# A planned kernel that counts TensorE's instructions in blocks of 256 and takes values in two stretches of a batch

## The chip, the core and the metric

One of the eight cores of one Trainium2 chip runs the kernel. The metric is the device time in microseconds; before, three runs took 1141.72, 1147.73 and 1151.67 us, with a median of 1147.73. The engines are TensorE (PE, its weight loads PEld), VectorE (DVE), ScalarE (ACT), GpSimd (POOL), and SyncE (SP), whose queue issues nearly all transfers.

## The reference

Attention with two mixings of heads, then two perceptrons. All arrays are float32 apart from the perceptrons' weights, which are float64 and are cut to float32 on the chip.

```python
scores = scale * np.matmul(q, k.transpose(0, 1, 3, 2))      # 4 batches, 12 heads, 448 x 448, depth 64
scores = np.einsum('bhij,hg->bgij', scores, w_pre)          # first mixing
attn = softmax(scores)                                      # with its maximum, + 1e-9 below
attn = np.einsum('bhij,hg->bgij', attn, w_post)             # second mixing
x = (attn @ v) -> (1792, 768)
h = x @ w_in; x = (h * np.cos(h)) @ w_out                   # 768 -> 2048 -> 768
h = max(x @ w1, x @ w2, x @ w3); out = h @ w_out2           # 768 -> 768 -> 768
```

## The kernel before, in words

**Attention.** A batch's 448 query rows are cut into groups of 12, 12, 11 and 10 "slots" of 10 rows. For each group and each of six head pairs TensorE makes products of queries and keys (`qk`, L587) into two PSUM banks; VectorE or ScalarE copies each to SBUF (`evac`, L486), and SP sends it (`send`, L608) into a grid `t` in which heads lie along partitions. A "visit" is two slots of this grid: the first mixing (`mix1`, L617), the maximum (`rowmax`, L625, VectorE), the exponential (`soft`, L631, ScalarE), the reciprocal of the sum (L636, L640), the scaling of w_post by it (`wscale`, L645), the second mixing (`mix2`, L655) of 56 narrow matmuls in the trace, and a copy (`keep`, L486) of its result for each slot into `a2`. When all visits of one or more groups have been kept (a "half" in `HALVES`), TensorE multiplies them with the values, two head pairs at a time (`av`, L682 and L684: one take), VectorE adds the two parts (`addx`, L703), and SP writes them to `xT` in memory (`out`, L707). Every float32 matmul of the program is two weight loads and two matmuls in the trace, every fp32r matmul one and one.

**Perceptrons.** Weights are rebuilt from float64 (L259 to L270) and, as `xT` is, split into two fp32r parts (L135, L138, L150, L154); three matmuls (L163 to L165) make each product. The first layer of batch 0 may run among the last visits.

**What sets the order.** `attention` adds every step to a `Plan` with a rank, a time on each engine that may do it, what must come before it, and which buffers it takes. `Plan.run` (L393) is a list scheduler: it keeps a clock for each engine, looks at all steps whose predecessors are placed, takes of those that can start within `WAIT` = 0.034 us of the earliest the one with the lowest rank, and writes its instructions at once. The order of every engine's queue is therefore fixed when the program is built, and each engine works through its queue in that order. Before, a step on TensorE can start when TensorE is free and its inputs are there, and nothing else counts.

The lines that say which groups of slots share a half, batch by batch, and the ranks of a half's takes:

```python
HALVES = [[[10], [12], [12, 11]], [[10, 12], [12, 11]], [[10, 12], [12, 11]], [[12, 11], [12], [10]]]
...
r = last + RAV + RAVGAP * x * APO / 2
...
soon = min(c)[0] + WAIT
t, rank, n, key = min((x for x in c if x[0] <= soon), key=lambda x: x[1:3])
```

## Time and profile before

| | us |
|---|---|
| median of three runs | 1147.73 |
| profiled execution | 1149.56 |
| its span, first to last instruction | 1147.8 |
| TensorE busy (matmuls) | 1102.0 (96%) |
| VectorE busy | 932.4 (81%) |
| ScalarE busy | 670.1 (58%) |

The granted TensorE clock was 0.995 of full speed. Each engine works on its own queue, so a wait costs time only if it lies on the chain that ends last. A matmul's busy time overlaps that of its neighbours: what a group costs is read from the start of its first matmul to the start of what follows. "issue" as the cause of a wait means that the engine waited for nothing that the profile shows.

### The profile page before, as it was taken

How to read it: one execution, taken by the hardware profiler on the slowest of the kernel's cores; microseconds unless marked ns; L12 is line 12 of the kernel's file. 1: busy time of each engine (PE TensorE's matmuls, PEld its weight loads, DVE VectorE, ACT ScalarE, POOL GpSimd, SP SyncE). 2: the span in 40 equal slices, each digit the busy share in tenths (PEclk: the TensorE clock that was granted, in tenths of full speed). 3: DMA queues.
4: the chain of work that ended last, by engine and by line, in shares of the span. 5: the costliest groups of instructions: out<-in, count | busy, mean ns of one | idle time of the engine just before them, and what ended most of it. 6: DMA issues, size and time to landing. Idle time of an engine off the chain costs nothing.

```text
span 1147.8 us, 30574 instructions
## 1 busy us (share of the span) xinstructions
PE 1102.0 (96%) x12332; PEld 943.5 (82%) x12332; DVE 932.4 (81%) x2011; ACT 670.1 (58%) x1477; POOL 56.5 (5%) x51
## 2 busy tenths in 40 slices
PE   9789989999988999999999999999999999999998
PEld 4566657666766899999999999999999999999987
DVE  5778868887879999897979798956977779778994
ACT  4667757766767985555555555545634354445472
POOL 4000000000000000000000000000001021011120
PEclk9999999999999999999999999999999999999999
DMA  6675755765544765343535353300012211222233
GB/s 213 204 204 173 217 168 173 217 210 168 173 147 136 260 188 171 117 151 104 151 104 152 92 147 101 123 21 22 1 53 67 74 49 40 78 63 70 83 119 115
DMA packets 96365, 146.89 MB, mean 128 GB/s; under 512 B 12672, under 2 KB 78816, under 8 KB 96224
## 3 DMA queue, kind: packets, MB, share of 16 engines
q1 hardware_dynamic: 95968, 144.92, 41.6%
q8 instruction: 97, 1.59, 0.6%
q14 instruction: 44, 0.36, 0.1%
q0 software_dynamic: 256, 0.02, 0.0%
HBM read 85.74 MB, written 20.45 MB: 93 GB/s over the span
## 4 chain that ended last, share of the span: by engine, by line
PE 85%; DVE 5%; DMA 4%; issue 3%; ACT 2%; SPq 0%; ACTq 0%; DVEq 0%
PE ps L164 21%; PE ps L165 21%; PE ps L163 21%; PE aps L655 6%; PE ps L587 6%; PE mps L617 5%; PE aps L682 4%; DMA t<-s 1%; DMA v<-in_v_dram 1%; DVE x L336 1%; DVE nm L625 1%; PE aps L684 1%; DMA wraw<-in_w_dram 0%; DVE xs L703 0%; DMA q<-in_q_dram 0%
## 5 line engine op out<-in xcount | busy, mean ns | idle before, releaser
L165 PE MATMUL ps<-x,w 128*128 128x448 f32 x816 | 299.8, 367 | 5.7 <-DVE x L154 5.5
L163 PE MATMUL ps<-x,w 128*128 128x448 f32 x816 | 300.0, 368 | 1.8 <-ACT x L150 0.7
L164 PE MATMUL ps<-x,w 128*128 128x448 f32 x816 | 299.2, 367 | 0.4 <-DVE w L299 0.3
L165 PEld LDWEIGHTS ps<-x,w 128*128 128x128 f32 x816 | 153.2, 188 | 22.3 <-DVE x L154 9.0
L163 PEld LDWEIGHTS ps<-x,w 128*128 128x128 f32 x816 | 153.2, 188 | 16.8 <-ACT gh L925 1.0
L164 PEld LDWEIGHTS ps<-x,w 128*128 128x128 f32 x816 | 153.2, 188 | 14.2 <-DVE w L299 1.1
L631 ACT ACTIVATE e<-mps,nm 128x448 f32<-128x448 f32 (+1 forms) x184 | 115.4, 637 | 44.3 <-DVE nm L625 41.0
L163 PE MATMUL ps<-gh,w 128*128 128x448 f32 x384 | 140.9, 367 | 0.0
L164 PE MATMUL ps<-gh,w 128*128 128x448 f32 x384 | 140.7, 366 | 0.0
L165 PE MATMUL ps<-gl,w 128*128 128x448 f32 x384 | 140.5, 366 | 0.0
L655 PEld LDWEIGHTS aps<-w2s,e 60*64 60x64 f32 x5040 | 95.9, 135 | 41.1 <-issue 27.1
L296 ACT CAST w<-wf 128x384 fp32r<-128x384 f32 x168 | 81.2, 514 | 73.7 <-DVE wf L288 50.8
L625 DVE TENSOR_REDUCE nm<-mps 128x1 f32<-128x448 f32 (+1 forms) x184 | 108.0, 614 | 19.1 <-PE mps L617 18.0
L655 PE MATMUL aps<-w2s,e 60*64 60x60 f32 x5040 | 99.4, 220 | 21.3 <-issue 19.7
L587 PE MATMUL ps<-k,q 64*64 64x448 f32 (+3 forms) x768 | 101.8, 550 | 4.9 <-DMA q<-in_q_dram 2.0
L617 PE MATMUL mps<-t,w 64*64 64x448 f32 (+1 forms) x720 | 100.7, 562 | 4.4 <-issue 4.0
L882 DVE TENSOR_TENSOR acc<-ps,acc 128x448 f32<-128x448 f32 x168 | 100.2, 614 | 4.8 <-PE ps L165 4.8
L299 POOL TENSOR_TENSOR w<-wf,w 128x384 fp32r<-128x384 f32 x36 | 42.7, 1195 | 1060.6 <-ACT w L296 1037.2
L259 ACT ACTIVATE wf<-wraw 128x384 f32<-128x384 f32 x112 | 61.1, 551 | 56.1 <-DMA wraw<-in_w_dram 28.5
L299 DVE TENSOR_TENSOR w<-wf,w 128x384 fp32r<-128x384 f32 x132 | 74.5, 584 | 19.0 <-ACT w L296 17.9
L682 PE MATMUL aps<-a,v 64*64 64x230 f32 (+3 forms) x1440 | 77.9, 317 | 2.0 <-DMA v<-in_v_dram 1.7
L165 PEld LDWEIGHTS ps<-gl,w 128*128 128x128 f32 x384 | 72.1, 188 | 6.5
(116 smaller groups left out, 1722.3 us busy)
## 6 DMA issues: line engine op xcount, KB each, us to landing
t<-s SPq DMA_DIRECT2D x96, 210.0 KB
wf<-w SPq DMA_DIRECT2D x96, 192.0 KB
wraw<-in_w_out_dram SPq DMA_DIRECT2D x44, 384.0 KB
wraw<-in_w_dram SPq DMA_DIRECT2D x36, 384.0 KB
wraw<-in_w_in_dram SPq DMA_DIRECT2D x32, 384.0 KB
t<-s SPq DMA_DIRECT2D x48, 192.5 KB
w<-wf SPq DMA_DIRECT2D x48, 192.0 KB
t<-s SPq DMA_DIRECT2D x42, 175.0 KB
```

Source lines behind the costliest of these rows:

```text
L163: mm(w[0], x[0], start=first, stop=False)
L164: mm(w[1], x[0], start=False, stop=False)
L165: mm(w[0], x[1], start=False, stop=last)
L296: return nc.scalar.copy(A[x][0], w())
L299: return eng.tensor_sub(A[x][1], w(), f32(A[x][0]))
L587: nc.tensor.matmul(live["s", n, 2 * hp + g][r:end], live["q", b, x, hp][half, i0 + r:i0 + end], live["k", b, hp][half], start=True, stop=True)
L617: nc.tensor.matmul(live["m", v, a][64 * y:64 * y + 64], w1[k], grids[n % 2][k, t + y, :], start=True, stop=True)
L625: nc.vector.tensor_reduce(nm, of(v, live["m", v, a]), axis=AX.X, op=ALU.max, negate=True)
L631: nc.scalar.activation(of(v, e), of(v, live["m", v, a]), AF.Exp, bias=live["nm", v, a], scale=1.0, accum_out=live["z", v][:, a:a + 1])
L655: nc.tensor.matmul(live["a", v, y][64 * c:64 * c + 64, u], live["e", v, a][k, j * JC:j * JC + JC], live["w2s", v][k, a], start=True, stop= ...
L682: nc.tensor.matmul(to, live["v", b, hp][k, j, g, :], rows[:, 2 * j - 2:2 * j], start=j == 1, stop=j == JP)
L882: return nc.vector.tensor_add(acc, po, acc) if fg else nc.scalar.copy(acc, po)
```

## The change

The plan gets a count of TensorE's instructions. `COUNT` says how many a step has (a second mixing of two slots 112, a take of values 128, a product of queries and keys or a first mixing 16, a perceptron step 6 to 18). `fetched` holds the count so far and a time: whenever a placed step reaches the next multiple of 256, that time becomes the moment of the crossing plus `FETCH` = 4.2 us. A step that would cross the next multiple before then is given a later start (`stop`), so that a step that does not cross, or crosses later, can come before it. Waits that stand in TensorE's queue as instructions of their own are not counted. Besides, `HALVES` joins the group of 10 slots with that of 12 in batches 0 and 3, so that every batch has two halves; there are 24 takes of values instead of 30.

```diff
@@ -24,7 +24,7 @@
 JP = JB // 2
 IBLK = [(0, S)]
 QG = 1
-HALVES = [[[10], [12], [12, 11]], [[10, 12], [12, 11]], [[10, 12], [12, 11]], [[12, 11], [12], [10]]]
+HALVES = [[[10, 12], [12, 11]], [[10, 12], [12, 11]], [[10, 12], [12, 11]], [[12, 11], [12, 10]]]
 
 NHALF = 230
 LOAD = 5.0
@@ -37,6 +37,8 @@
 WAIT = 0.034
 APO = 2
 LEFT = 4
+CHUNK, FETCH = 256, 4.2
+COUNT = {"qk": 16, "stir": 8, "mix1": 16, "mix2": 112, "av": 64 * APO, "hidden": 6, "product": 12, "unit_product": 18}
 RAV, RAVGAP, AVY, RMIX2, RKEEP, RQK, RQKGAP = 2.5, 3.0, 2, 1.5, 1.5, -2.5, 0.1
 KC = DM // 128
 KH = KC // 2
@@ -399,6 +401,13 @@
                 users.setdefault(x, []).append(key)
         order = {key: n for n, key in enumerate(self.ops)}
         self.banks, holder, closed = {}, [None] * places["bank"], set()
+
+        fetched = [CHUNK // 4, -50.0]
+
+        def stop(key, t):
+
+            b, n = CHUNK - fetched[0] % CHUNK, COUNT.get(key[0], 6)
+            return max(0.0, fetched[1] - t - self.ops[key][2]["T"] * b / n) if b <= n else 0.0
 
         def bank_free(x):
             if holder[x] is None:
@@ -432,7 +441,10 @@
                     best.setdefault("-", []).append((t, rank, order[key], key))
                     continue
                 start, eng = min((max(free[e], t) + d , e) for e, d in engines.items())
-                best.setdefault(eng, []).append((max(free[eng], t), rank, order[key], key))
+                t = max(free[eng], t)
+                if eng == "T":
+                    t += stop(key, t)
+                best.setdefault(eng, []).append((t, rank, order[key], key))
             assert best, [(k, [x for x in self.ops[k][3] if x not in done]) for k in list(open_)[:9]]
             picks = []
             for eng, c in best.items():
@@ -453,6 +465,11 @@
                 done[key] = t
             else:
                 d = engines[eng]
+                if eng == "T":
+                    b, n = CHUNK - fetched[0] % CHUNK, COUNT.get(key[0], 6)
+                    if b <= n:
+                        fetched[1] = t + d * b / n + FETCH
+                    fetched[0] += n
                 free[eng] = t + d
                 done[key] = t + d + (self.lands[key] or self.LATENCY[eng])
             handle = run(eng)
```

**Where it moves work.** In TensorE's queue in batch 1, the last take of values of the groups of 10 and 12 slots (`aps<-a` with `v`) and what follows it, before; L587 is a product of queries and keys, L617 a first and L655 a second mixing:

```order
L617 MATMUL mps<-t,w_139 64x448 x4
L682 MATMUL aps<-a_2261,v_145 64x220 x4
L684 MATMUL aps<-a_2261,v_145 64x110 x4
L682 MATMUL aps<-a_2261,v_145 64x220 x8
L682 MATMUL aps<-a_2261,v_146 64x220 x4
L684 MATMUL aps<-a_2261,v_146 64x110 x4
L682 MATMUL aps<-a_2261,v_146 64x220 x8
L655 MATMUL aps<-w2s,e 64x60 x84
L617 MATMUL mps<-t,w_139 64x448 x4
L587 MATMUL ps<-k,q 64x448 x2
```

The same take now (L604 is a product, L634 a first and L672 a second mixing, L699 and L701 are values):

```order
L634 MATMUL mps<-t,w_139 64x448 x4
L699 MATMUL aps<-a_2096,v_145 64x220 x4
L701 MATMUL aps<-a_2096,v_145 64x110 x4
L699 MATMUL aps<-a_2096,v_145 64x220 x8
L699 MATMUL aps<-a_2096,v_146 64x220 x4
L701 MATMUL aps<-a_2096,v_146 64x110 x4
L699 MATMUL aps<-a_2096,v_146 64x220 x8
L672 MATMUL aps<-w2s,e 64x60 x28
L634 MATMUL mps<-t,w_139 64x448 x4
L604 MATMUL ps<-k,q 64x448 x2
L604 MATMUL ps<-k,q 56x448 x2
L672 MATMUL aps<-w2s,e 64x60 x56
```

Before, three second mixings (x84) stand right behind the values; now one does, and a first mixing and a product stand between it and the next two.

The first take of values of batch 0, before (it is of the 10 slots alone, and its second mixings follow):

```order
L587 MATMUL ps<-k,q 64x448 x2
L587 MATMUL ps<-k,q 56x448 x2
L682 MATMUL aps<-a_483,v_142 64x100 x4
L684 MATMUL aps<-a_483,v_142 64x50 x4
L682 MATMUL aps<-a_483,v_142 64x100 x8
L682 MATMUL aps<-a_483,v_143 64x100 x4
L684 MATMUL aps<-a_483,v_143 64x50 x4
L682 MATMUL aps<-a_483,v_143 64x100 x8
L655 MATMUL aps<-w2s,e 64x60 x56
L617 MATMUL mps<-t,w_139 64x448 x8
```

The same place now:

```order
L604 MATMUL ps<-k,q 64x448 x2
L604 MATMUL ps<-k,q 46x448 x2
L634 MATMUL mps<-t,w_139 64x448 x4
L699 MATMUL aps<-a_483,v_142 64x220 x4
L701 MATMUL aps<-a_483,v_142 64x110 x4
L699 MATMUL aps<-a_483,v_142 64x220 x8
L699 MATMUL aps<-a_483,v_143 64x220 x4
L701 MATMUL aps<-a_483,v_143 64x110 x4
L699 MATMUL aps<-a_483,v_143 64x220 x8
L672 MATMUL aps<-w2s,e 64x60 x28
```

The take has 220 columns instead of 100; ahead of it stand eleven second mixings instead of five, and behind it one instead of two.

The end of the attention in TensorE's queue, the first take of values after the last second mixing, before (L163 to L165 are the perceptrons' matmuls):

```order
L163 MATMUL ps<-x,w 128x448
L164 MATMUL ps<-x,w 128x448
L165 MATMUL ps<-x,w 128x448
L682 MATMUL aps<-a_7266,v_146 64x100 x4
L684 MATMUL aps<-a_7266,v_146 64x50 x4
L682 MATMUL aps<-a_7266,v_146 64x100 x8
L682 MATMUL aps<-a_7266,v_147 64x100 x4
L684 MATMUL aps<-a_7266,v_147 64x50 x4
L682 MATMUL aps<-a_7266,v_147 64x100 x8
L163 MATMUL ps<-x,w 128x448
```

And now (L165 to L167 are the perceptrons' matmuls):

```order
L165 MATMUL ps<-x,w 128x448
L166 MATMUL ps<-x,w 128x448
L167 MATMUL ps<-x,w 128x448
L699 MATMUL aps<-a_6566,v_146 64x220 x4
L701 MATMUL aps<-a_6566,v_146 64x110 x4
L699 MATMUL aps<-a_6566,v_146 64x220 x8
L699 MATMUL aps<-a_6566,v_147 64x220 x4
L701 MATMUL aps<-a_6566,v_147 64x110 x4
L699 MATMUL aps<-a_6566,v_147 64x220 x8
L165 MATMUL ps<-x,w 128x448
```

These last takes have 220 columns instead of 100. From the first matmul after the attention's last take to the end, TensorE's queue has the same 3781 rows before and now.

## Rows read from the trace of the kernel before

**Rows 1.** Page, busy us (share of the span) x instructions of each engine

```profile
PE 1102.0 (96%) x12332; PEld 943.5 (82%) x12332; DVE 932.4 (81%) x2011; ACT 670.1 (58%) x1477; POOL 56.5 (5%) x51
```

**Rows 2.** Busy time by stage; columns: stretch us, engines' busy us (x instructions), clock, DMA

```profile
45.00:311.00 266.00, 242.81 (x6590) 176.28 (x6586) 214.43 (x592) 182.46 (x479) 0.00 (x0) 0.99 0.62 189
311.00:365.00 54.00, 45.67 (x1305) 37.33 (x1298) 42.41 (x119) 38.82 (x94) 0.00 (x0) 0.97 0.50 152
365.00:390.00 25.00, 21.67 (x97) 17.44 (x97) 23.10 (x49) 20.26 (x42) 0.00 (x0) 1.00 0.75 253
390.00:1148.00 758.00, 753.13 (x3684) 690.96 (x3683) 625.59 (x1184) 404.38 (x808) 42.73 (x36) 1.00 0.32 96
```

**Rows 3.** Who ended TensorE's waits, 45 to 365: us in total, times, longest

```profile
PE aps L655 <- issue: 19.7, 18, 4.1
PE mps L617 <- issue: 4.0, 3, 2.1
PE ps L165 <- DVE x L154: 3.0, 2, 1.6
...
PE ps L587 <- issue: 0.8, 1, 0.8
...
PE aps L682 <- issue: 0.3, 1, 0.3
```

**Rows 4.** Chain of waits, 45 to 365 us: shares of its length by line

```profile
by line: PE aps L655 21.3%; PE mps L617 19.3%; PE ps L587 18.0%; PE aps L682 13.8%; issue 8.8%; DVE nm L625 2.2%; PE aps L684 1.9%; DMA t<-s 1.9%; DMA v<-in_v_dram 1.4%; DVE xs L703 1.4%; ACT e L631 1.2%; DMA wraw<-in_w_out_dram 1.2%; ACT x
```

**Rows 5.** Page, DMA queues: packets, MB, share of 16 engines

```profile
q8 instruction: 97, 1.59, 0.6%
```

**Rows 6.** Busy times between ends of successive issue waits, columns as in rows 2

```profile
62.28:68.24 5.96, 5.17 (x127) 3.29 (x127) 4.93 (x12) 3.45 (x10) 0.00 (x0) 1.00 0.58 170
68.24:73.12 4.88, 4.56 (x127) 3.52 (x127) 3.56 (x11) 2.66 (x7) 0.00 (x0) 1.00 0.73 211
...
175.82:178.85 3.03, 2.49 (x137) 2.36 (x128) 2.40 (x9) 2.62 (x8) 0.00 (x0) 1.00 0.41 142
324.82:331.91 7.09, 3.03 (x137) 2.89 (x129) 3.17 (x13) 3.46 (x10) 0.00 (x0) 0.99 0.73 230
```

**Rows 7.** Timeline of TensorE from 36 us: start, us, engine, line, tiles, count

```profile
36.52 1.02 PE L655 MATMUL aps<-w2s,e 60*64 60x60 f32 x56
37.34 0.96 PE L587 MATMUL ps<-k,q 64*64 64x448 f32 x8
38.09 0.96 PE L617 MATMUL mps<-t,w 64*64 64x448 f32 x8
38.85 1.71 PE L587 MATMUL ps<-k,q 64*64 64x448 f32 x16
```

**Rows 8.** Timeline of TensorE, takes of values: first row of each and what follows it

```profile
323.26 0.62 PE L682 MATMUL aps<-a,v 64*64 64x230 f32 x8
...
325.99 1.86 PE L655 MATMUL aps<-w2s,e 60*64 60x60 f32 x102
...
335.32 0.39 PE L682 MATMUL aps<-a,v 64*64 64x120 f32 x8
...
336.79 0.94 PE L617 MATMUL mps<-t,w 64*64 64x448 f32 x8
...
358.74 0.41 PE L682 MATMUL aps<-a,v 64*64 64x100 f32 x8
...
360.18 0.47 PE L163 MATMUL ps<-x,w 128*128 128x448 f32 x1
```

**Rows 9.** Helpers by line, 45 to 311 us: busy us, mean ns, idle before

```profile
L625 DVE TENSOR_REDUCE nm<-mps 128x1 f32<-128x448 f32 (+1 forms) x152 | 89.4, 613 | 7.7 <-PE mps L617 6.7
L486 DVE COPY s<-ps 120x448 f32<-120x448 f32 (+2 forms) x82 | 49.0, 616 | 5.9 <-PE ps L587 3.5 <-DMA t<-s 2.0
...
L631 ACT ACTIVATE e<-mps,nm 128x448 f32<-128x448 f32 (+1 forms) x152 | 95.4, 638 | 39.2 <-DVE nm L625 36.0 <-DVE rz L640 2.9 <-DVE z L636 0.2
L486 ACT COPY a<-aps 128x420 f32<-128x420 f32 x92 | 48.3, 563 | 24.0 <-PE aps L655 23.6
```

## The prediction, made before the changed kernel ran

> **What bounds the kernel now.** First the page's busy times: TensorE (PE) is busy 1102.0 of 1147.8 us, VectorE (DVE) 932.4, ScalarE (ACT) 670.1 [rows 1]. An average over the span hides where the 46 us of TensorE's idle time lie, so next the busy times by stage [rows 2]. From 390 us to the end TensorE works 753.1 of 758 us: the perceptrons have nothing to give. In the attention from 45 to 311 us it works 242.8 of 266 us, in the last softmaxes and values from 311 to 365 us 45.7 of 54. VectorE has 214.4 busy us in the former stretch, 81%, and is no bound there; from 365 to 390 us it has 23.1 of 25 and is one.

> Next, who ends TensorE's waits from 45 to 365 us [rows 3]: not another engine but "issue", a wait for nothing that the profile shows, 19.7 + 4.0 + 0.8 + 0.3 = 24.8 us in 18 + 3 + 1 + 1 = 23 waits. The largest wait with another name is 3.0 us. The chain of waits says that these are on the path: 8.8% of its length in this stretch is "issue" [rows 4], 28 us of 320.

> **The change, part by part.** *The count in the plan.* It changes no duration and inserts no wait; it changes the order in which the planner puts work, on TensorE and in consequence on VectorE, ScalarE and SP. I price an order by cutting it into stretches of 256 instructions as the trace does. A float32 matmul of the order is two matmuls and two loads, four instructions, a perceptron matmul two. Prices, start to start [rows 7]: a second mixing of 56 matmuls (112 instructions) 0.82 us, a product of queries and keys and a first mixing of 8 matmuls (16 instructions) 0.75 and 0.76. A take of values of two head pairs, 64 matmuls (128 instructions), took 2.73 us at 230 columns, 1.47 at 120 and 1.44 at 100 [rows 8]. So 256 instructions of second mixings are 1.9 us of work, of products and first mixings 12. Walking both orders with the separate waits counted, from 31 us to the last value: before 65 stretches, of which 22 hold under 3.25 us of work and 13 hold 3.25 to 4.6; changed 62, of which 12 and 27. The reason is visible in the order: before, 20 of 28 groups of values have two or three second mixings right behind them, now 3 of 22, and products and first mixings stand between.

> What that saves: if the 24.8 us of waits belong to the 22 short stretches, they are 1.13 us each, and ten fewer save 11.3 us. If instead every stretch lasts at least 3.6 us (the floor that gives 26.8 us with the order of before, near the 24.8 measured), the changed order keeps 9.8 of 26.8 and saves 17. I take **13**, nearer to the first, because the 27 middling stretches will stop sometimes: in the first and second stretch of [rows 6], 5.17 and 4.56 us of busy time took 5.96 and 4.88 us.

> [...]

> *The values in two stretches.* In batches 0 and 3 the scores of 10 and of 12 slots share one take. The columns stay the same, the takes fall from 30 to 24. A take at 220 columns is 2.73 x 220/230 = 2.61 us against 1.47 + 1.44 [rows 8]: 0.30 less, for 3 takes in 2 batches **1.8 us**. The 768 instructions that go are the three stretches fewer that are counted above. Copies of values fall by 6, stores to xT from 60 to 48 of twice the size; VectorE and SP are not late here, and I cost these at nothing. VectorE's cover is the 19% of its time that it has free in 45 to 311 us [rows 2].

> *The start.* The first values now come after 11 second mixings instead of 5. In the six between, TensorE has 6 x 0.82 + 8 x 0.76 + 7 x 0.75 = 16.2 us of other work, and before it had three takes of values more and a fourth just behind, 4 x 1.44 = 5.8 us. The two helpers need for it at least 16 maxima and 16 exponentials, 12 copies of mixings and 14 of scores, 16 x (0.613 + 0.638) + 12 x 0.563 + 14 x 0.616 = 35.4 us [rows 9], 17.7 each, and small ones besides. So TensorE starves here a little, and the four takes come later, where it is full. Cost 0 (the takes fill stops that there would be) to 5.8 (all are added): I take **3**. What is late next is the mixing behind VectorE's maxima.

> *The end.* Before, the values of 12 slots stand among the last mixings (335 to 347 us), and only 100 columns, 3 x 1.44 = 4.3 us, come after the last one. Now 220 columns come after it, 7.8 us. The stretch of the last mixings is set by VectorE, which makes softmax, the parts of x and of weights there (waits on x L154 [rows 3]), so what leaves it leaves a hole. Cost 0 (while TensorE takes values, VectorE prepares batch 1's x, whose waits from 365 us on go away) to 3.5: I take **2**.

> *Behind it.* From the first matmul after the last value TensorE's order is the same row for row: 0.

> Sum: -13 - 1.8 + 3 + 2 = -9.8. The profiled execution took 1149.56 us (span 1147.8 and 1.8 around it), so 1139.8 against it. It lies 1.8 us above the median of the three runs, 1147.73, so for a median **1138 us**; with the bounds of each term (-17 - 1.8 to -11.3 - 1.8 + 9.3) 1129 to 1144.

> **Rivals.** *Nearly all stops go.* For it: the groups with two and more mixings behind values almost vanish. Against it: twelve stretches under 3.25 us are left, and the plan does not count the separate waits in TensorE's queue (217 up to the last value in the program before, 177 now), so that its count is most of a block off by the end. It gives -24.8 - 1.8 + 5 = -21.6, 1126 us. 0.12.

> *The stops stay.* A block is late because its packet starts late, behind data on the DMA engines (7.09 us for the one stretch), or the waits move into the middling stretches; then only values, start and end are left: -1.8 + 5 = +3.2, 1151 us. Against it: 10 of 22 short stretches are gone, and a stretch with more work needs a later packet to stop. 0.20. [...]

> *TensorE starves through batch 0: slower.* If VectorE and ScalarE set the pace from 40 us until batch 0's last values, at (17.7 - 16.2)/6 = 0.25 us for each second mixing at least, and twice that with the small instructions, 22 mixings cost 5.5 to 11 us, and saved stops are worth nothing where TensorE waits anyhow. With the end's 3.5: +11 - 1.8 + 3.5 = +12.7 less a rest of the saving, about 1158 us at worst. It decides as soon as the waits of first and second mixings on VectorE in 40 to 120 us pass 13 us. Against it: VectorE has 19% free, and copies can go to either helper. 0.08.

> The forecast itself: 0.60. Its own range is 1129 to 1144. A difference of 1% (11.5 us) is about what a measurement of this kernel can tell from none; the three runs lie within 10 us. Faster by over 1% means under 1136.3: the first rival and not quite half of the forecast, 0.40. Within 1%: the rest of the forecast and most of the second rival, 0.51. Slower: 0.09. The range that should hold the time is 1126 to 1150: it reaches to the first rival and nearly to the second.

> **What would show it.** In the changed profile "issue" waits of TensorE from 45 us to the last value should be about 12 us, in some 12 to 16 waits; the last value should end near 355 instead of 364.5 us; from 390 us on nothing should differ. The start is right if waits on VectorE or ScalarE of 1 to 4 us appear between 40 and 70 us; the end if waits on x L154 shrink from 365 us on. It is wrong if "issue" stays above 20 us, or if the attention's last value comes earlier and the perceptrons do not.

## The result, and the profile after

The changed kernel takes 1134.9 us (median of 4 runs, 1132.23 to 1136.46) against 1148.35 before (4 runs of the same chip): a ratio of 0.9888, with a 95% interval of 0.9839 to 0.9936. The profiled execution took 1132.23 us, the fastest of the four, with a span of 1130.4. It is 17.3 us shorter than the profiled one of before, and 4 us of that are the luck of the two draws. In the ratios and intervals below, though not in the medians, executions clearly longer than the others of their kernel are left out; the longest, 2180.7 us, is one of 12 of the kernel with the waits counted.

The page's busy times and the queue of instructions, after (they answer to [rows 1, 5]):

```profile
PE 1096.7 (97%) x11948; PEld 942.8 (83%) x11948; DVE 930.5 (82%) x2009; ACT 669.5 (59%) x1473; POOL 56.7 (5%) x51
...
q8 instruction: 94, 1.54, 0.6%
```

TensorE has 384 matmuls and as many loads fewer, the six takes of values that are gone, and three instruction packets fewer. Busy times by stage, the borders put where the same work ends, but for the first, which is 45 us in both (by then the changed kernel has 80 matmuls of first mixings behind it instead of 56; answers to [rows 2]):

```profile
45.00:297.00 252.00, 234.61 (x6372) 173.73 (x6366) 209.92 (x585) 178.11 (x470) 0.00 (x0) 0.99 0.66 200
297.00:348.00 51.00, 45.52 (x1140) 37.88 (x1134) 44.91 (x122) 40.87 (x97) 0.00 (x0) 0.97 0.50 159
348.00:374.00 26.00, 23.20 (x110) 18.93 (x105) 22.33 (x49) 20.61 (x44) 0.00 (x0) 1.00 0.70 240
374.00:1131.00 757.00, 751.61 (x3678) 689.72 (x3676) 624.19 (x1180) 404.14 (x805) 42.93 (x36) 1.00 0.31 96
```

The stretch from 45 us to the last product of queries and keys is 14 us shorter (252 instead of 266), the one up to the last value 3 us (51 instead of 54); from the last value on the two differ by less than 2 us. The last value ends at 348.1 us instead of 364.4. Of these 16 us, 11.3 are idle time of TensorE (26.1 us from the start to the last value instead of 37.4) and 4.9 are busy time (322.1 instead of 327.0), part of it the six takes that are gone.

Who ended TensorE's waits from 45 us to the last value, after (us in total, times, longest; answers to [rows 3]; "issue" stands in two rows, the others are waits on other engines and transfers):

```profile
PE aps L672 <- issue: 4.9, 4, 2.2
PE aps L672 <- DVE w2s L662: 4.3, 5, 1.9
PE ps L167 <- DVE x L156: 2.6, 3, 1.6
PE aps L699 <- issue: 2.0, 2, 1.1
PE aps L672 <- ACT a L503: 1.9, 2, 1.3
PE ps L604 <- DMA t<-s: 1.7, 1, 1.7
PE mps L634 <- DMA t<-s: 1.4, 2, 1.2
PE mps L634 <- ACT a L503: 1.3, 1, 1.3
PE aps L699 <- ACT s L503: 1.2, 1, 1.2
```

Issue waits are 4.9 + 2.0 = 6.9 us in 6 waits instead of 24.8 in 23. But waits on VectorE, ScalarE and transfers, which were 3.0 + 1.9 + 1.2 + 0.4 = 6.5 us before (the first in [rows 3]), are now 4.3 + 2.6 + 1.9 + 1.7 + 1.4 + 1.3 + 1.2 = 14.4 us in these rows, and 15.6 with the small ones that are not shown.

Not all of these are what the view calls them. In the trace of before, every one of the 23 issue waits ends 1.3 to 1.6 us after a packet of 16 KB of the instruction queue has ended, and stands at the same place, give or take one instruction, in a block of 256 instructions: 193 or 194 loads, matmuls and separate waits behind a multiple of 256. Three waits of after that the view puts down to others stand within two places of it (194, 195 and 196) and end 1.4 to 1.7 us after such a packet; for the first, the named cause had ended 0.69 us before, for the second, the transfer landed 0.01 us after the wait had ended, and for the third, where a transfer landed 0.04 us before, it may have been either:

```profile
126.17 0.96 PE L634 MATMUL mps<-t,w 64*64 64x448 f32 x5 [1.35 <-ACT a L503]
...
155.57 0.96 PE L604 MATMUL ps<-k,q 64*64 64x448 f32 x7 [1.66 <-DMA t<-s]
...
237.16 0.97 PE L634 MATMUL mps<-t,w 64*64 64x448 f32 x6 [1.21 <-DMA t<-s]
```

Before has one such, of 1.9 us, put down to values at 244.45 us. With them the stops went from 26.7 us in 24 waits to 11.1 in 9 (9.9 in 8 without the third), and the waits on other engines and transfers from 4.6 to 11.4 us.

The chain of waits shows the shift too (answers to [rows 4]): "issue" 5.9% instead of 8.8, and DMA, ACT and DVE are on it where second mixings were.

```profile
by line: PE aps L672 14.8%; PE mps L634 13.6%; PE aps L699 11.8%; PE ps L604 11.3%; DMA t<-s 9.9%; issue 5.9%; ACT e L648 4.0%; DVE nm L642 3.6%; DVE s L503 3.1%; DMA k<-in_k_dram 2.5%; DMA x<-xT 2.4%; DVE xs L720 2.0%; PE aps L701 1.8%; DM
```

### The profile page after: what moved, and what is told of

Same layout as the page of the kernel before. It is cut to its first block, busy times and chain, and to the rows that moved or that the text cites. A ratio compares the mean times of both kernels' runs of the same rounds, so it can differ in the third digit from the quotient of the medians.

```text
span 1130.4 us, 29730 instructions
## 1 busy us (share of the span) xinstructions
PE 1096.7 (97%) x11948; PEld 942.8 (83%) x11948; DVE 930.5 (82%) x2009; ACT 669.5 (59%) x1473; POOL 56.7 (5%) x51
## 4 chain that ended last, share of the span: by engine, by line
PE 84%; DMA 7%; DVE 5%; ACT 2%; issue 2%; SPq 0%; DVEq 0%; ACTq 0%
PE ps L165 22%; PE ps L167 22%; PE ps L166 22%; PE ps L604 4%; PE aps L672 4%; PE mps L634 4%; PE aps L699 3%; DMA t<-s 3%; DVE nm L642 1%; DMA wraw<-in_w_in_dram 1%; ACT e L648 1%; DVE s L503 1%; DMA k<-in_k_dram 1%; DMA x<-xT 1%; DVE xs L720 1%
## 5 line engine op out<-in xcount | busy, mean ns | idle before, releaser
L167 PE MATMUL ps<-x,w 128*128 128x448 f32 x816 | 299.8, 367 | 4.3 <-DVE x L156 4.1
L165 PE MATMUL ps<-x,w 128*128 128x448 f32 x816 | 299.9, 368 | 1.8 <-ACT x L152 1.1
L167 PEld LDWEIGHTS ps<-x,w 128*128 128x128 f32 x816 | 153.2, 188 | 21.0 <-DVE x L156 7.7
L165 PEld LDWEIGHTS ps<-x,w 128*128 128x128 f32 x816 | 153.2, 188 | 17.2 <-ACT x L152 1.6
L166 PEld LDWEIGHTS ps<-x,w 128*128 128x128 f32 x816 | 153.2, 188 | 13.9 <-DVE w L301 0.7
L165 PE MATMUL ps<-gh,w 128*128 128x448 f32 x384 | 140.8, 367 | 0.0
L167 PE MATMUL ps<-gl,w 128*128 128x448 f32 x384 | 140.4, 366 | 0.0
L672 PEld LDWEIGHTS aps<-w2s,e 60*64 60x64 f32 x5040 | 98.7, 136 | 35.7 <-issue 16.9
L672 PE MATMUL aps<-w2s,e 60*64 60x60 f32 x5040 | 100.4, 220 | 12.4 <-issue 5.4
L634 PE MATMUL mps<-t,w 64*64 64x448 f32 (+1 forms) x720 | 95.6, 553 | 4.2 <-DMA t<-s 1.7
L604 PE MATMUL ps<-k,q 64*64 64x448 f32 (+3 forms) x768 | 96.8, 557 | 2.0 <-DMA t<-s 1.7
L167 PEld LDWEIGHTS ps<-gl,w 128*128 128x128 f32 x384 | 72.1, 188 | 6.5
L165 PEld LDWEIGHTS ps<-gh,w 128*128 128x128 f32 x384 | 72.1, 188 | 6.2
```

The costliest lines, as they stand in the source:

```text
L165: mm(w[0], x[0], start=first, stop=False)
L166: mm(w[1], x[0], start=False, stop=False)
L167: mm(w[0], x[1], start=False, stop=last)
L604: nc.tensor.matmul(live["s", n, 2 * hp + g][r:end], live["q", b, x, hp][half, i0 + r:i0 + end], live["k", b, hp][half], start=True, stop=True)
L634: nc.tensor.matmul(live["m", v, a][64 * y:64 * y + 64], w1[k], grids[n % 2][k, t + y, :], start=True, stop=True)
L672: nc.tensor.matmul(live["a", v, y][64 * c:64 * c + 64, u], live["e", v, a][k, j * JC:j * JC + JC], live["w2s", v][k, a], start=True, stop= ...
```

## The experiments

Theory A, with which I came out of the prediction: a stop comes wherever a block of 256 instructions held too little work, so the time follows the number of such blocks, which depends on the order and on where the blocks' edges happen to fall in it. Rivals: the halves earn the gain; or the count earns it, because the plan knows where the edges are. "Floor" below is what blocks of less than 3.6 us lack, summed over the real order, as in the prediction.

All waits of the table are TensorE's from 15 to 400 us in one profiled execution of the kernel, summed over the causes in the view of waits ("other" are those on other engines and transfers); the ratio is to the kernel before, run beside it (its medians were 1145.9 to 1148.4).

| kernel | floor us | issue us (waits) | other waits us | median us | ratio, 95% |
|---|---|---|---|---|---|
| before | 26.9 | 24.8 (23) | 13.9 | 1145.9 to 1148.4 | 1 |
| before, edges moved 160 | 13.3 | 21.4 (18) | 13.6 | 1140.9 | 0.9954 (0.9919 to 0.9989) |
| two halves, no count | 11.7 | 5.8 (6) | 18.9 | 1134.7 | 0.9892 (0.9849 to 0.9936) |
| two halves, no count, moved 160 | 28.8 | 22.9 (15) | 9.8 | 1138.9 | 0.9945 (0.9913 to 0.9978) |
| count, old halves | 11.9 | 15.7 (16) | 12.1 | 1139.3 | 0.9965 (0.9935 to 0.9994) |
| the change | 9.8 | 7.4 (8) | 19.1 | 1134.9 | 0.9888 (0.9839 to 0.9936) |
| the change, moved 160 | 9.7 | 3.4 (5) | 24.6 | 1134.7 | 0.9910 (0.9881 to 0.9939) |
| the change, count half a block off | 13.3 | 9.1 (13) | 16.5 | 1135.1 | 0.9919 (0.9885 to 0.9954) |
| count, three halves in batch 0 | 12.3 | 8.0 (11) | 14.5 | 1138.0 | 0.9936 (0.9906 to 0.9966) |
| count, three halves in batch 3 | 9.9 | 5.5 (5) | 25.7 | 1138.1 | 0.9948 (0.9920 to 0.9975) |
| the change, waits counted | 9.5 | 2.6 (3) | 28.2 | 1141.9 | 0.9975 (0.9945 to 1.0005) |
| waits counted, 5.0 us a block | 9.0 | 3.4 (4) | 24.3 | 1142.5 | 0.9987 (0.9959 to 1.0015) |

A profiled execution can lie at either end of its kernel's runs: that of the two halves without the count took 1140.8 us, the slowest of 7 runs, and that with three halves in batch 0 took 1131.6, the fastest of 12. So the waits are compared by their kinds, the times by the medians. Counted by place and packet instead of by the name "issue", before has 26.7 us of stops in 24 waits, the change 11.7 in 11, and the kernel with three halves in batch 3 has 8.3 in 7; the other rows move by 1 us at most. The floor ranks the orders only roughly: before with moved edges has 21.4 us of issue waits where it gives 13.3, the two halves without the count 5.8 where it gives 11.7.

**Do the edges decide?** The first try put the same order behind a block of tiny matmuls at the start:

```diff
-    for _ in range(2):
+    for _ in range(1):
         nc.tensor.matmul(begun[:64], w1[:64], ...[:, :S], start=True, stop=True)
+    for _ in range(41):
+        nc.tensor.matmul(begun[:64, :8], w1[:64], ...[:, :8], start=True, stop=True)
```

> The kernel before with its order unchanged on every engine, but for one of the two idle matmuls at the start, which is replaced by 41 tiny ones: all later instructions of TensorE stand 160 places further back against the blocks of 256. Theory A (a stop comes where a block of 256 instructions held little work; what counts is where the blocks' edges fall): a floor of 3.6 us for each block gives 13.3 us of stops instead of 26.9, so about 13 us faster, 1135 us, and issue waits of about 10 us on TensorE from 45 us on. Rival B (the gain of the change comes from its order and its fewer takes, and edges do not matter): 1148 us and 25 us of issue waits as before.

It took 1147.5 us, ratio 1.0015 (0.9985 to 1.0046). The timeline of TensorE at its start (start, duration, count) shows why this says nothing:

```profile
3.28 8.86 PE L506 MATMUL mps<-v,w 64*64 64x8 f32 x82
12.20 8.34 PE L589 MATMUL ps<-k,q 64*64 64x448 f32 x64
```

The 82 small matmuls, all on one set of rows, took 8.9 us, and the first products began at 12.20 instead of 5.04 us. The same edit on the two halves without the count has the same flaw:

> The two halves without the count, and TensorE's instructions 160 places further back as in the shifted kernel before. Theory A: now 28.8 us of stops instead of 11.7, so 15 to 17 us slower than the halves alone, about 1150 us. Rival B (edges do not matter): the same time as the halves alone.

It took 1146.0 us, 0.9996 (0.9964 to 1.0028), of which some 7 are the lost start. So both were made again, with the tiny matmuls alternating between row halves and banks:

```diff
+    both = begun, bank_pools[1].tile([128, 512], F32, tag="bank", name="mps")[:, :S]
+    for n in range(41):
+        a, c = n % 2, n // 2 % 2
+        nc.tensor.matmul(both[a][64 * c:64 * c + 64, :8], w1[64 * a:64 * a + 64], ...[64 * a:...][:, :8], start=True, stop=True)
```

> The shifted kernel before once more, with the 41 tiny matmuls spread over two halves of TensorE's rows and two banks, so that they cost little at the start (the 82 of the first try took 8.9 us there and put the first scores 7.5 us back). The order behind them is that of before. Theory A (edges of the blocks decide): the first try had 18.0 us of issue waits instead of 24.8, and the floor of 3.6 us gives 13.6 us less, so 7 to 13 us faster than before, 1134 to 1140 us. Rival B (edges shift stops about but the path gets no shorter): 1145 to 1149 us.

1140.9 us, ratio 0.9954. The same order is 5 us faster, less than the 7 to 13 expected, for nothing but where the blocks' edges fall (the first products begin at 5.79 us here, 0.75 later than before). That the edges make the stops is shown directly: counting loads, matmuls and separate waits in this trace, every wait on "issue" over 0.3 us stands 193 or 194 places behind a multiple of 256, as all 23 do in the kernel before, in front of other instructions. TensorE's largest issue groups from 45 to 365 us here:

```profile
PE aps L660 <- issue: 16.7, 13, 4.1
PE aps L687 <- issue: 2.6, 2, 1.7
```

The expected 10 us of issue waits did not come: they are 21.4 us, 3.4 less than before. This profiled execution is the slowest of its 12 (1148.2 us), so the 5 us stand on the medians and the interval, not on this trace.

**The halves alone, at two places of the edges.** The edit is the line `HALVES` of the change, and nothing else.

> The two halves of every batch without the count in the plan. Theory A: a floor of 3.6 us a block gives 11.7 us of stops by the luck of where the edges fall, 15 fewer than before; less 1.8 for the takes and up to 5 more at the start and end: 1133 to 1138 us, hardly other than the change. Rival B (the count in the plan earns the gain): no more than the takes' 1.8 us, 1146 to 1151 us.

1134.7 us: the whole gain of the change without its count, at this place of the edges. With the edges moved:

> Two halves in every batch, no count, TensorE's instructions 160 places further back by cheap tiny matmuls. Theory A: 28.8 us of stops by the floor instead of 11.7, so well slower than the halves alone (1134.7): 1145 to 1151 us. Rival E (what the halves bring is not a matter of edges: six takes fewer, and TensorE free for scores early on): within 3 us of 1135.

1138.9 us, 4 us slower, against 10 to 16 that Theory A asked for. TensorE's issue waits from 45 to 365 us in the two, first the halves alone:

```profile
PE aps L655 <- issue: 5.6, 5, 2.0
```

and moved:

```profile
PE aps L660 <- issue: 19.3, 11, 2.9
PE mps L622 <- issue: 2.3, 2, 1.8
```

The stops came back as the floor says (5.8 us to 22.9 from 15 to 400 us), but only a quarter of them shows in the time: the other waits fell from 18.9 to 9.8. A likely reading, not tested by itself, is that a stop lets VectorE, ScalarE and SP catch up, so that TensorE then does not wait for them. With nearly as many stops as before the halves are still 7 us faster than it. But against the order of before with its edges moved as well (21.4 us of stops, 1140.9 us) they are only 2 us faster, and the intervals overlap almost wholly. So that the halves bring something that is no matter of edges is not shown.

**The count alone.** `COUNT` and `stop` as in the change, `HALVES` as before.

> The count in the plan with the halves of before (30 takes). Theory A: 11.9 us of stops instead of 26.9, and no cost at the start and end: 1133 to 1136 us. Rival C (the fewer takes and instructions earn the gain): about 1148 us.

1139.3 us, ratio 0.9965. By its ratio the count alone earns 4 us, by the medians 7, and so a third to a half of the change; my 1133 to 1136 was too good.

**Must the plan know where the edges are?** Two kernels put its count out by half a block or more: one moves the real edges, one starts the count elsewhere (`fetched = [CHUNK // 4 + CHUNK // 2, -50.0]`).

> The changed kernel with TensorE's instructions 160 places further back by cheap tiny matmuls, so that its plan's count is off by more than half a block. Theory A: the floor gives 9.7 us of stops instead of 9.8, because the spread order has few short blocks wherever the edges fall: 1135 us, no change. Rival F (the count works because the plan knows where the edges are): 5 to 10 us slower, 1140 to 1145 us.

> The changed kernel, but the plan's count starts 128 later, so that it spaces work about edges that lie half a block from the real ones. Theory A: 13.3 us of stops by the floor instead of 9.8, so 1135 to 1139 us. Rival F (the plan must know where the edges are): the gain over the halves alone turns into a loss, 1140 us or more. Rival E (the halves bring all): 1135 us.

1134.7 and 1135.1 us, both the same as the change. The rival that the plan has to know the edges falls. What the count does is to place a product or a first mixing between values and second mixings often, and by the floor that serves wherever the edges are: the change's order has 7.5 to 11.4 us of floor in all of eight places of the edges that I counted, the order of the halves alone 10.3 to 28.8, and the order of before about 14 to 27, so that before stands near its worst place. The times agree at the moved place: the change 1134.7 us, the halves alone 1138.9, the order of before 1140.9, three kernels that ran side by side. At the first place the halves alone are as fast as the change. So what the count adds to the halves is that the gain no longer hangs on where the edges fall, as far as two places, and intervals that overlap a little, can show it.

**Where do the halves help?**

> The count in the plan; batch 0 keeps its three halves of before (first values after 5 second mixings), batch 3 has two. Theory G (joining the halves of batch 0 brings most: less is taken from TensorE early, the scores of the next groups go out sooner, and the values come where there is room): about as slow as the count alone, 1137 to 1140 us. Theory H (the prediction's term for the start: 3 us lost by two halves there): 1131 to 1134 us.

> The count in the plan; batch 0 has two halves, batch 3 keeps its three (values of 12 slots among the last mixings, 100 columns behind the last one). Theory G: as the change, 1134 to 1136 us. Theory H (the prediction's term for the end: 2 us lost by two halves there): 1132 to 1134 us. If the end is what the two halves help: 1138 to 1140 us.

`HALVES` is that of the change but for its first or its last entry. 1138.0 and 1138.1 us: by the medians each join is worth some 3 us. Their intervals overlap that of the change and that of the count alone, so this is likely and not shown. The runs do speak against the charge of the prediction, by which one join less would have made the kernel 2 to 3 us faster than the change, and neither was. Each join moves the edges as well: by the floor that is worth 2.5 us in batch 0 and nothing in batch 3.

**A better count.** The plan counts the separate waits as well, then also allows 5.0 us a block:

```diff
-COUNT = {"qk": 16, "stir": 8, "mix1": 16, "mix2": 112, "av": 64 * APO, ...}
+COUNT = {"qk": 16.5, "stir": 8, "mix1": 16.65, "mix2": 112.65, "av": 64 * APO + 0.4, ...}
-        fetched = [CHUNK // 4, -50.0]
+        fetched = [72, -50.0]
```

> The changed kernel whose plan also counts the separate waits in TensorE's queue, as a mean for each step (0.65 for a mixing, 0.5 for a product, 0.4 for a take), from a start that matches the real queue. Theory A with what the moved runs showed (stops are no longer the bound once the order is spread): 9.5 us of stops by the floor instead of 9.8, so 1133 to 1136 us, no change. Rival F (the plan must know where the edges are): 3 to 6 us faster, 1129 to 1132 us.

> The kernel with the waits counted, and 5.0 instead of 4.2 us as the time that the plan allows a block. Spreads a little more: 9.0 us of stops by the floor. Theory A with saturation: 1132 to 1136 us. If the plan's time were what is off: 1130 us or below.

1141.9 and 1142.5 us: 7 us slower than the change, with the fewest issue waits of all, 2.6 and 3.4 us. Neither theory had this. TensorE's waits of the kernel with the waits counted, 45 to 365 us:

```profile
PE ps L165 <- DVE xs L720: 4.4, 1, 4.4
PE mps L634 <- DMA v<-in_v_dram: 4.1, 2, 2.2
PE aps L672 <- DVE w2s L662: 2.9, 5, 1.0
PE mps L634 <- ACT xl L503: 2.8, 1, 2.8
PE aps L672 <- issue: 2.6, 3, 1.5
PE ps L604 <- DMA k<-in_k_dram: 2.4, 2, 2.0
```

Issue is the second smallest of these rows; transfers of values and keys, the additions of values and the scaled weights hold TensorE instead (28.2 us of waits on other engines and transfers from 15 to 400 us, against 19.1 in the change by the same count). Why these plans' orders wait more elsewhere was not tested. No version beat the change.

## Why the prediction was right, step by step

**The bound: right.** The stops at every 256th instruction and the rest of the program were as read: the perceptrons did not move (751.6 busy us instead of 753.1 in the last stretch), and moved edges moved the stops (5.8 us to 22.9 with the two halves) and the time (1134.7 to 1138.9). How much of a stop lies on the path was read too high, see the next term. That a part of it does lie there is shown by the same order, which gained 5 us by moved edges alone (1140.9 us, ratio 0.9954).

**The count, 13 us saved (11.3 to 17).** In stops, 26.7 - 11.1 = 15.6 us went from 45 us to the last value, inside the range (24.8 - 6.9 = 17.9 by the name "issue" alone), and the 11.1 us in 9 waits are near the 12 us in 12 to 16 waits that were named as the sign. In time it was less: some 7 us came back as waits on other engines and transfers. Three things were missing in the term. It took a stop for a loss of its full length, and the halves with and without moved edges show that 17 us of stops cost 4. It gave to the count what the halves do to the order as well: the halves alone have about as few short blocks as the change, where the edges happen to lie. And it took the edges as given, though 5 us of the gain could be had with the order of before by moving them.

**The takes, 1.8 us saved.** A take at 220 columns took 338.51 to 341.30 and 342.71 to 348.14 for two, so 2.7 to 2.8 us; 2.61 was predicted. Six takes at 0.1 to 0.2 us more leave 0.7 to 1.2 of the 1.8. The timeline of TensorE at the end of the attention, after:

```profile
335.51 1.04 PE L672 MATMUL aps<-w2s,e 60*64 60x60 f32 x56
...
338.51 0.61 PE L699 MATMUL aps<-a,v 64*64 64x220 f32 x8
...
341.30 0.47 PE L165 MATMUL ps<-x,w 128*128 128x448 f32 x1
...
342.71 0.61 PE L699 MATMUL aps<-a,v 64*64 64x220 f32 x8
...
347.23 0.98 PE L699 MATMUL aps<-a,v 64*64 64x220 f32 x16
348.14 0.47 PE L165 MATMUL ps<-x,w 128*128 128x448 f32 x1
```

**The start, 3 us lost: failed.** The step that failed is "So TensorE starves here a little, and the four takes come later, where it is full." Busy times from 42 to 70 us, before and then after:

```profile
42.00:70.00 28.00, 23.20 (x740) 17.91 (x744) 18.30 (x53) 14.59 (x39) 0.00 (x0) 0.94 0.64 187
```

```profile
42.00:70.00 28.00, 26.20 (x764) 19.31 (x761) 25.01 (x75) 21.87 (x59) 0.00 (x0) 1.00 0.75 223
```

TensorE does more in the same 28 us (26.20 against 23.20), and VectorE and ScalarE far more (25.01 and 21.87 against 18.30 and 14.59). Its waits from 40 to 72 us, after:

```profile
PE aps L672 <- issue: 1.8, 2, 1.4
PE mps L634 <- DMA t<-s: 0.2, 1, 0.2
PE ps L604 <- DMA k<-in_k_dram: 0.2, 1, 0.2
```

None is on VectorE or ScalarE. I set the helpers' 17.7 us against TensorE's 16.2 and forgot the order's other side: before, the early values stood ahead of products and first mixings, and the two helpers had idle time for want of them. Values feed nobody but the additions; products feed everyone. Part of the difference is stops: of TensorE's waits from 40 to 72 us 4.5 us were issue before, and the clock was 0.94 of full. With the count and three halves in batch 0 the stretch holds this:

```profile
42.00:70.00 28.00, 25.93 (x806) 20.52 (x806) 21.46 (x63) 18.58 (x51) 0.00 (x0) 0.94 0.65 193
```

TensorE is as busy as after, and the helpers lie halfway (21.46 and 18.58): about half of what they gained goes with the joined halves. Keeping the three halves in batch 0 was 3 us slower by the medians, and not 3 faster.

**The end, 2 us lost: half right.** From the last first mixing to the last value it is 24.2 us (324.0 to 348.2) instead of 21.4 (343.0 to 364.4): 2.8 us more, as said. But the stretch ahead of it, from the last product to the last first mixing, is 27.2 us (296.8 to 324.0) instead of 32.4, one stop of 4.06 us among them (a stretch at a clock of 0.50 lies in both). The sign came weakly: waits on x L154 from 365 us on fell from 2.5 to 1.5 us, and one of 1.1 us on the other part of x (L152, 0.7 before) stands beside them. In the median the three halves in batch 3 are no better.

**The sum** of -9.8 met -13.4 by errors of both signs: the count was given more than it has of its own, the halves less. That the number came so near is in part luck. Faster by over 1% was given 0.40, and 1.1% came; the rival of nearly no stops, 1126 us, was near on the stops (7 to 11 us left) and wrong on the time, because the waits changed their cause.

**Left open.** How many us each join earns by its fewer instructions, by the edges and by the start cannot be told apart: the joins change all three, and 12 runs of a kernel still spread over 9 to 16 us.

## What to carry to other kernels

A stop like those here is found by counting: if waits on "issue" repeat at a fixed number of instructions (all 23 of the kernel before stand 193 or 194 places behind a multiple of 256), look for the places where many short instructions stand together, and put long ones between. Move the edges once by cheap instructions before crediting an order with a gain, since the same order differed by 4 to 5 us here. Look at the place in the block and at the queue's packets too, since the view of waits put such a stop down to another cause in two or three of the 9 waits of the change. And waits that go from a queue need not show in the time, because others can come in it: two plans with less than half of the change's issue waits (2.6 and 3.4 us instead of 7.4) were 7 us slower, with 28.2 and 24.3 us of other waits instead of 19.1.

## What was not expected of the hardware

Beside some stops the granted clock was half. It is shown here for the three attention stretches of before in which it was not full (columns as in [rows 2], the clock is the last but two):

```profile
48.51:51.92 3.41, 3.41 (x51) 2.49 (x47) 2.65 (x5) 1.66 (x5) 0.00 (x0) 0.50 0.67 209
154.32:157.73 3.41, 3.41 (x25) 1.30 (x21) 3.06 (x9) 2.45 (x7) 0.00 (x0) 0.50 0.86 237
331.82:335.23 3.41, 3.32 (x26) 1.55 (x29) 2.09 (x4) 1.85 (x4) 0.00 (x0) 0.50 0.17 32
```

Each comes with an issue wait of 2.15, 2.06 or 4.06 us (the others were 1.9 us or less), from 0.9 us behind its end to just before it, and is a stretch of 3.41 us at 0.50 of full: about 1.7 us of lost work each, as an estimate (half of 3.41). In the third, two first mixings took 2.9 us (332.39 to 335.32) where they otherwise take 1.5. After, the wait of 2.20 us that ended at 74.89 us did the same:

```profile
74.68:78.10 3.42, 3.21 (x26) 1.90 (x30) 1.22 (x2) 1.10 (x2) 0.00 (x0) 0.50 0.74 191
...
320.42:323.84 3.42, 3.42 (x78) 2.42 (x75) 1.94 (x5) 2.29 (x5) 0.00 (x0) 0.50 0.55 160
```

The second of these came behind two waits of 1.26 and 0.71 us, while in before the waits of 1.58 us that ended at 62.28 and of 1.91 us that ended at 244.45 were followed by the full clock, 1.00 from 51.92 to 154.32 and from 157.73 to 331.82 us. So the length of one wait did not tell whether the clock fell, and what does is open.

The prediction had no term for it. Before had three such stretches in the attention and after two, so little of it is in the difference of the two traces. The mean granted clock differs between executions of the kernel before, from 0.987 to 1.000, and that goes with part of the spread of 9 to 16 us among 12 runs of one order: over 25 to 31 runs of the kernel before in each set of experiments, the longer ones had the lower granted clock (correlation -0.51 to -0.77, 0.8 to 1.1 us for 0.001 of the clock).
